# Linear attention with two expert layers on one core: the decay of the state moved from GpSimd to VectorE

## The chip, the cores and the metric

One core of a Trainium2 chip runs the whole program. A core has TensorE (PE in the profile; its weight loads are PEld), VectorE (DVE), ScalarE (ACT), GpSimd (POOL) and SyncE (SP, which issues the DMAs here). Each engine works through its own queue in order; semaphores tie the queues together. The metric is device time in microseconds, the median of several runs.

## What is computed

A linear attention with a complex, decaying state, then two expert layers on its output:

```python
for t in range(S):                      # q, k, v, a_re, a_im: [4, 8, 768, 48]
    ar, ai = a_re_n[:, :, t, :, None], a_im_n[:, :, t, :, None]
    new_re = ar * S_re - ai * S_im
    new_im = ar * S_im + ai * S_re
    kv = einsum('bhd,bhe->bhde', k[:, :, t], v[:, :, t])
    S_re, S_im = new_re + kv, new_im
    y[:, :, t] = einsum('bhd,bhde->bhe', q[:, :, t], S_re)
x = y.transpose(0, 2, 1, 3).reshape(3072, 384)
x = (silu(x @ w_gate) * (x @ w_val)) @ w_out      # 384 -> 1536 -> 384
h = x @ w_in                                      # 384 -> 2048
out = (h - tanh(h)) @ w_out2                      # -> 384
```

`a_re_n`, `a_im_n` are the inputs with their magnitude capped at 0.999.

## The kernel before

The 768 steps of each of the 4 batches are cut into 6 chunks of 128 steps. A batch and a chunk are a unit; there are 24, numbered 0 to 23, and chunk 0 of a batch begins with an empty state. Decay factors are prepared for two units at a time (`group_steps`: the magnitude's norm, a running complex product within the chunk on VectorE by `cstep`, L278 to L281, and at the end the small tile `LS` with the decay from one chunk's reference point to the next). `unit_a` scales q and k by the running products and sends them through DRAM to have them by head (`TQ`, `TK`). `unit_b` computes the unit's output: scores (`psS`, L434), the mask (L438 or L440), the outputs (`psY`: L462 with the scores, L466 with the state `Hn`), and the new state.

The state lies in a tile of 96 partitions: 48 rows of the real part, 48 of the imaginary part, and 384 columns (8 heads of 48). The step from one chunk to the next multiplies each row by the real factor of the decay, and adds the swapped halves (real and imaginary exchanged) times the imaginary factor. So a unit that is not the last of its batch computes `psG` (L446, what its keys and values add), adds the state it came with (L449 on VectorE; in chunk 0 ScalarE copies, L451) and gets `Z`; two DMAs on SP's queue (L453, L454) write `Z` with its halves exchanged into `Zs`. The next unit turns `Z` and `Zs` into `Hn` on GpSimd:

```python
POOL.tensor_tensor(out=heads(Hn), in0=heads(Z), in1=lam(0), op=ALU.mult)   # L427
POOL.tensor_tensor(out=heads(Zs), in0=heads(Zs), in1=lam(1), op=ALU.mult)  # L428
POOL.tensor_tensor(out=Hn, in0=Hn, in1=Zs, op=ALU.add)                     # L429
```

20 of the 24 units do that. `Z`, `Zs` and `Hn` have one buffer each, so a new `Hn` also waits for the matmuls that read the old one. GpSimd has besides these only the mask of the first eight units (L438) and two operations of the norm for ten groups (L241, L262).

The first expert layer (`moe1_tile`) runs over tiles of 2, 2, 2, 3, 3, 4, 4 and 4 units, each in 12 steps: 9 gate matmuls and 9 value matmuls (L581), silu on ScalarE (L585), the product (L590) and the split into a rounded part and a rest (L540 on ScalarE, L541 on VectorE), and 9 matmuls of `w_out` (L565). A tile can start when the outputs of its units are there. These steps are interleaved with attention. The second layer (`moe2_tile`, L645 and L668) comes after it and has TensorE for itself. Weights are decoded from 64-bit words by ScalarE and VectorE (L144 to L156).

The kernel is written in an order that mixes the steps by hand, and a scheduler then sets each engine's order by a simulated time line. So an edit of one operation can move others on all engines.

## Time and profile before

| | |
|---|---|
| median of 3 runs | 1235.29 us (1232.09 to 1238.32) |
| profiled execution | 1236.95 us, its span 1235.2 us |
| TensorE busy | 1091.5 us, 88% |
| VectorE busy | 985.6 us, 80% |
| ScalarE busy | 656.3 us, 53% |
| GpSimd busy | 128.2 us, 10% |
| mean granted clock of TensorE | 0.942 |

Busy shares are averages over stages with different limits, so they are read by stretch: attention and the first layer mixed (to about 640 us), the first layer's last tiles with little attention left (to about 740), then the rest of the first layer with the decode of the second layer's weights, and from about 850 us the second layer alone. An idle engine costs nothing where another sets the end; the chain of work that ended last tells which engine was waited for.

### The profile page before, as it was taken

What the parts mean: (1) busy time and instruction counts of PE and PEld (TensorE: products, weight loads), DVE (VectorE), ACT (ScalarE), POOL (GpSimd) and SP (SyncE); (2) the same over time, 40 slices, a digit from 0 to 9 for tenths busy, and PEclk for the clock granted to TensorE, in tenths of its full rate; (3) what the DMA queues carried; (4) which work ended last, traced back from release to release, by engine and by line L of the source; (5) the groups of instructions that cost most, each with busy time, mean ns of one, the idle gap of its engine ahead of it and who ended that gap; (6) DMA issues with size and microseconds to landing.
All of it is one profiled execution on the core that took longest, in us unless ns stands there. A gap on an engine that the chain in (4) does not pass through costs nothing.

```text
span 1235.2 us, 18483 instructions
## 1 busy us (share of the span) xinstructions
PE 1091.5 (88%) x6504; PEld 973.1 (79%) x6504; DVE 985.6 (80%) x2010; ACT 656.3 (53%) x1247; POOL 128.2 (10%) x110
## 2 busy tenths in 40 slices
PE   3157847879989999889999999989999999999997
PEld 1145847879988888878878888878999999999997
DVE  4888968866969778596885338989888888888886
ACT  5446537466464754536535224565565655555553
POOL 0011322202212122021111000000000000000000
PEclk9568977999989999889999999999999999999999
DMA  6397777897985978687667658652100102020000
GB/s 154 76 214 162 177 159 199 210 202 194 216 195 141 191 183 188 153 212 156 145 166 180 161 138 284 215 159 90 51 27 24 54 1 77 1 77 1 26 2 28
DMA packets 296707, 163.36 MB, mean 132 GB/s; under 512 B 157472, under 2 KB 273824, under 8 KB 296608
## 3 DMA queue, kind: packets, MB, share of 16 engines
q1 hardware_dynamic: 296608, 162.11, 52.3%
q8 instruction: 53, 0.87, 0.3%
q14 instruction: 46, 0.38, 0.1%
HBM read 111.82 MB, written 37.86 MB: 121 GB/s over the span
## 4 chain that ended last, share of the span: by engine, by line
PE 53%; DVE 17%; DMA 13%; ACT 9%; issue 3%; SPq 3%; POOL 0%; DVEq 0%; ACTq 0%
PE l L645 16%; PE l L668 15%; PE l L581 10%; PE acc L565 5%; DMA TQ<-qk_d 3%; PE psS L434 3%; DVE prod L278 3%; DVE PL L280 1%; DMA raw<-in_moe_w_out_dram 1%; DMA qk_d<-QK 1%; DMA TK<-qk_d 1%; PE psG L446 1%; DVE lo L541 1%; DVE t L590 1%; ACT PL L271 1%
## 5 line engine op out<-in xcount | busy, mean ns | idle before, releaser
L581 PE MATMUL l<-x,wgv 128*128 128x256 f32 (+2 forms) x1728 | 351.0, 350 | 10.8 <-ACT t L585 9.3
L581 PEld LDWEIGHTS l<-x,wgv 128*128 128x128 f32 x1728 | 284.8, 196 | 40.0 <-ACT t L585 12.7
L668 PE MATMUL l<-x,wi 128*128 128x512 f32 x864 | 215.1, 394 | 5.1 <-DVE t L611 5.1
L645 PE MATMUL l<-w,hi 128*128 128x384 f32 x768 | 189.7, 337 | 0.0
L668 PEld LDWEIGHTS l<-x,wi 128*128 128x128 f32 x864 | 161.9, 189 | 35.1 <-DVE t L611 6.2
L565 PE MATMUL acc<-hi,wo 128*128 128x256 f32 (+2 forms) x576 | 167.3, 351 | 9.1 <-ACT wo L154 4.1
L540 ACT CAST hi<-t 128x512 fp32r<-128x512 f32 (+2 forms) x192 | 108.6, 566 | 118.3 <-DVE t L590 87.4
L645 PEld LDWEIGHTS l<-w,hi 128*128 128x128 f32 x768 | 140.9, 189 | 7.4
L541 DVE TENSOR_TENSOR lo<-t,hi 128x512 fp32r<-128x512 f32 (+2 forms) x192 | 123.7, 645 | 26.7 <-ACT hi L540 26.5
L604 ACT ACTIVATE t<-l 128x512 f32<-128x512 f32 x96 | 57.3, 597 | 147.1 <-PE l L668 143.0
L645 PE MATMUL l<-w,lo 128*128 128x384 f32 x384 | 122.3, 337 | 0.0
L565 PEld LDWEIGHTS acc<-hi,wo 128*128 128x128 f32 x576 | 106.0, 196 | 20.1 <-ACT wo L154 5.1
L278 DVE TENSOR_TENSOR prod<-PL 128x384 f32<-128x384 f32 x168 | 104.8, 624 | 2.7
L565 PE MATMUL acc<-lo,wo 128*128 128x256 f32 (+2 forms) x288 | 98.5, 346 | 0.0
L434 PE MATMUL psS<-TQ,TK 96*128 96x128 f32 x384 | 61.8, 316 | 37.3 <-DMA TQ<-qk_d 19.5
L606 DVE TENSOR_TENSOR l<-l,t 128x512 f32<-128x512 f32 x96 | 67.1, 698 | 33.4 <-ACT uu L605 33.2
L434 PEld LDWEIGHTS psS<-TQ,TK 96*128 96x128 f32 x384 | 57.3, 225 | 42.6 <-issue 28.8
L590 DVE TENSOR_TENSOR t<-t,l 128x256 f32<-128x256 f32 (+2 forms) x96 | 52.6, 547 | 32.5 <-PE l L581 18.4
L585 ACT ACTIVATE t<-l 128x256 f32<-128x256 f32 (+2 forms) x96 | 47.1, 491 | 48.9 <-PE l L581 46.4
L611 DVE COPY_PREDICATED t<-far,l 128x512 f32<-128x512 int32 x96 | 71.0, 740 | 2.6
L610 DVE SCALAR_TENSOR_TENSOR t<-vv,t 128x512 f32<-128x512 f32 x96 | 66.2, 689 | 6.8
L645 PEld LDWEIGHTS l<-w,lo 128*128 128x128 f32 x384 | 71.4, 188 | 0.2 <-DVE lo L541 0.2
(129 smaller groups left out, 1670.8 us busy)
## 6 DMA issues: line engine op xcount, KB each, us to landing
wo<-wo_d SPq DMA_DIRECT2D x84, 384.0 KB, 3.9
qk_d<-QK SPq DMA_DIRECT2D x24, 768.0 KB, 4.7
TK<-qk_d SPq DMA_DIRECT2D x48, 192.0 KB, 4.2
TQ<-qk_d SPq DMA_DIRECT2D x48, 192.0 KB, 4.9
x<-o_d SPq DMA_DIRECT2D x12, 768.0 KB, 5.9
x<-y SPq DMA_DIRECT2D x48, 144.0 KB, 4.3
raw<-in_moe_w_in_dram SPq DMA_DIRECT2D x16, 384.0 KB, 4.1
raw<-in_moe_w_out_dram SPq DMA_DIRECT2D x16, 384.0 KB, 3.4
```

What stands on the lines that cost most here:

```text
L278: DVE.tensor_tensor(out=pr, in0=prev.unsqueeze(2).to_broadcast(sh), in1=cur.unsqueeze(1).to_broadcast(sh), op=ALU.mult)
L434: PE.matmul(ps[:, P * i:P * (i + 1)], lhsT=TK[:, 4 * hh + i], rhs=TQ[:, 4 * hh + i], start=True, stop=True)
L540: ACT.copy(out=hi, in_=t)
L541: DVE.tensor_tensor(out=lo, in0=t, in1=hi.bitcast(F32), op=ALU.subtract)
L565: PE.matmul(acc[j], lhsT=w[:, a, j * P:(j + 1) * P], rhs=m[b], start=(f == 0 and i == 0), stop=(f == NF1 - 1 and i == 2))
L581: PE.matmul(p, lhsT=w[a][:, kk], rhs=x[b][:, kk, 0:n_t], start=(n == 0), stop=(n == 3 * NJ - 1))
L590: DVE.tensor_tensor(out=s, in0=s, in1=ps[1], op=ALU.mult)
L606: DVE.tensor_tensor(out=p, in0=p, in1=t, op=ALU.subtract)
L610: DVE.scalar_tensor_tensor(out=t, in0=vv, scalar=G_F, in1=t, op0=ALU.add, op1=ALU.mult)
L611: DVE.copy_predicated(out=t, mask=far, data=p)
L645: PE.matmul(acc[tb], lhsT=g[a][:, tb * P:(tb + 1) * P], rhs=w2_hl[f][:, b], start=(f == 0 and n == 0), stop=(f == NF2 - 1 and n == 2))
L668: PE.matmul(p, lhsT=wi_hl[a][:, kk, sl], rhs=x[b][:, kk, :], start=(n == 0), stop=(n == 3 * NJ - 1))
```

## The change

The two planes `Z` and `Zs` become halves of one tile `ZZ` of 96 x 2 x 384. VectorE multiplies both planes in one instruction, in place, with the two factors of `LS` spread over the columns, and adds the planes into `Hn` in a second one. GpSimd no longer takes part. The state's sum, ScalarE's copy and the two DMAs stay, with the halves of `ZZ` as their targets.

```diff
-            Z = st.pop("Z")
-            Zs = st.pop("Zs")
+            ZZ = st.pop("Z")
             Hn = a1.tile([D2, DM], F32, tag="H", name="Hn")
-            lam = lambda x: LS[:, :, x, g].unsqueeze(2).to_broadcast([D2, H, D])
-            POOL.tensor_tensor(out=heads(Hn), in0=heads(Z), in1=lam(0), op=ALU.mult)
-            POOL.tensor_tensor(out=heads(Zs), in0=heads(Zs), in1=lam(1), op=ALU.mult)
-            POOL.tensor_tensor(out=Hn, in0=Hn, in1=Zs, op=ALU.add)
+            z4 = ZZ.rearrange("p c (h d) -> p c h d", h=H)
+            DVE.tensor_tensor(out=z4, in0=z4, in1=LS[:, :, :, g].rearrange("p h c -> p c h").unsqueeze(3).to_broadcast([D2, 2, H, D]), op=ALU.mult)
+            DVE.tensor_tensor(out=Hn, in0=ZZ[:, 0], in1=ZZ[:, 1], op=ALU.add)
...
-            Z = a1.tile([D2, DM], F32, tag="Z", name="Z")
+            ZZ = a1.tile([D2, 2, DM], F32, tag="Z", name="Z")
+            Z, Zs = ZZ[:, 0], ZZ[:, 1]
             if c > 0:
                 DVE.tensor_tensor(out=Z, in0=Hn, in1=ps[0:D2, 0:DM], op=ALU.add)
             else:
                 ACT.copy(out=Z, in_=ps[0:D2, 0:DM])
-            Zs = a1.tile([D2, DM], F32, tag="Zs", name="Zs")
             SP.dma_start(out=Zs[0:D], in_=Z[D:D2])
             SP.dma_start(out=Zs[D:D2], in_=Z[0:D])
-            st["Z"], st["Zs"] = Z, Zs
+            st["Z"] = ZZ
```

In the new file the lines behind the edit carry smaller numbers: the product is L426, the sum L427, the state's sum L448, the first layer's product L588 and its split L539, y L470.

GpSimd's queue in the middle of attention, before (L241 and L262 belong to the norm):

```order
L262 TENSOR_TENSOR ar<-ar,s_4911 128x768
L428 TENSOR_TENSOR Zs<-Zs,LS 96x384
L427 TENSOR_TENSOR Hn<-Z,LS 96x384
L429 TENSOR_TENSOR Hn<-Hn,Zs 96x384
L241 TENSOR_TENSOR s_5307<-s_5307,s_5308 128x768
```

The same queue in the changed kernel:

```order
L241 TENSOR_TENSOR s_4889<-s_4889,s_4890 128x768
L262 TENSOR_TENSOR ar<-ar,s_4889 128x768
L241 TENSOR_TENSOR s_5281<-s_5281,s_5282 128x768
L262 TENSOR_TENSOR ar<-ar,s_5281 128x768
L241 TENSOR_TENSOR s_6025<-s_6025,s_6026 128x768
```

The decay is gone from it and only the norm is left.

VectorE's queue around the state's sum before the decay of unit 10, before (L278 to L281 are the scan, L590 and L541 the first layer):

```order
L449 TENSOR_TENSOR Z<-Hn,psG 96x384
L280 TENSOR_TENSOR PL<-prod 128x96
L281 TENSOR_TENSOR PL<-prod 128x96
L278 TENSOR_TENSOR prod<-PL 128x384
L590 TENSOR_TENSOR t<-t,l_4295 128x384
```

The same place in the changed kernel:

```order
L448 TENSOR_TENSOR Z<-Hn,psG 96x384
L588 TENSOR_TENSOR t<-t,l_4010 128x384
L539 TENSOR_TENSOR lo<-t,hi 128x384
L299 MEMSET PL 128x6
L278 TENSOR_TENSOR prod<-PL 128x384
L280 TENSOR_TENSOR PL<-prod 128x96
L281 TENSOR_TENSOR PL<-prod 128x96
L278 TENSOR_TENSOR prod<-PL 128x384
L426 TENSOR_TENSOR Z<-Z,LS 96x768
L280 TENSOR_TENSOR PL<-prod 128x96
L281 TENSOR_TENSOR PL<-prod 128x96
L427 TENSOR_TENSOR Hn<-Z 96x384
```

Product and sum now stand in VectorE's queue among the scan's steps, the product seven rows behind the state's sum.

VectorE's queue at the state's sum before the decay of unit 22, before:

```order
L449 TENSOR_TENSOR Z<-Hn,psG 96x384
L590 TENSOR_TENSOR t<-t,l_7394 128x512
L541 TENSOR_TENSOR lo<-t,hi 128x512
L472 TENSOR_TENSOR y<-psY,y 128x4x128
L590 TENSOR_TENSOR t<-t,l_7432 128x512
```

The same place in the changed kernel, with the semaphores each instruction waits for (DMAHW are DMA queues):

```order
L448 TENSOR_TENSOR Z<-Hn,psG 96x384 [waits PE_49]
L426 TENSOR_TENSOR Z<-Z,LS 96x768 [waits DMAHW3_49,DMAHW2_49,DMAHW4_49,DMAHW1_49,DVE_49]
L588 TENSOR_TENSOR t<-t,l_7392 128x512 [waits PE_49,Activation_49]
L539 TENSOR_TENSOR lo<-t,hi 128x512 [waits Activation_49]
L427 TENSOR_TENSOR Hn<-Z 96x384 [waits PE_49]
L470 TENSOR_TENSOR y<-psY,y 128x4x128 [waits DMAHW6_49,DMAHW3_49,DMAHW7_49,DMAHW0_49,Activation_49]
```

The product stands right behind the state's sum, ahead of the first layer's product and split.

## Rows read from the trace of the kernel before

**Rows 1.** The page: busy time of each engine, and the chain that ended last.

```profile
PE 1091.5 (88%) x6504; PEld 973.1 (79%) x6504; DVE 985.6 (80%) x2010; ACT 656.3 (53%) x1247; POOL 128.2 (10%) x110
...
PE 53%; DVE 17%; DMA 13%; ACT 9%; issue 3%; SPq 3%; POOL 0%; DVEq 0%; ACTq 0%
```

**Rows 2.** Busy time by stretch: length, engines (instructions), clock, DMA share, GB/s.

```profile
92.00:640.00 548.00, 474.84 (x3409) 435.77 (x3407) 441.53 (x1008) 304.73 (x603) 111.03 (x84) 0.93 0.77 181
640.00:850.00 210.00, 204.89 (x1068) 170.34 (x1067) 147.32 (x311) 93.67 (x173) 9.39 (x9) 0.98 0.64 187
```

**Rows 3.** Groups by line and shape: busy us, mean ns, idle before and releasers.

```profile
L390 DVE TENSOR_TENSOR QK<-qk,NW 128x768 f32<-128x768 f32 x48 | 47.1, 989 | 6.3 <-ACT qk L385 4.5 <-DMA qk_d<-QK 1.9
...
L427 POOL TENSOR_TENSOR Hn<-Z,LS 96x384 f32<-96x384 f32 x20 | 23.4, 1172 | 72.3 <-DVE prod L278 23.2 <-DMA LS<-lam_d 22.2 <-issue 13.3
...
L429 POOL TENSOR_TENSOR Hn<-Hn,Zs 96x384 f32<-96x384 f32 x20 | 22.6, 1130 | 1.5
...
L428 POOL TENSOR_TENSOR Zs<-Zs,LS 96x384 f32<-96x384 f32 x20 | 20.1, 1006 | 176.7 <-DMA Zs<-Z 143.8 <-DVE t L590 25.0 <-DVE T L335 7.7
...
L261 DVE SCALAR_TENSOR_TENSOR ai<-ai,sgn,s 128x768 f32<-128x768 f32 x12 | 17.2, 1430 | 0.0
...
L156 DVE TENSOR_TENSOR wi<-t,wi 128x384 fp32r<-128x384 f32 x16 | 8.8, 553 | 0.1
```

**Rows 4.** Instructions in order of time: start, duration, engine, line; VectorE beside GpSimd.

```profile
92.91 1.16 POOL L427 TENSOR_TENSOR Hn<-Z,LS 96x384 f32<-96x384 f32 x1
93.29 1.20 DVE L146 TENSOR_SCALAR dt<-dt 128x768 int32<-128x768 int32 x1
...
96.47 1.19 POOL L429 TENSOR_TENSOR Hn<-Hn,Zs 96x384 f32<-96x384 f32 x1
...
107.56 0.55 DVE L146 TENSOR_SCALAR dt<-dt 128x768 int32<-128x768 int32 x1
...
715.19 0.69 DVE L472 TENSOR_TENSOR y<-psY,y 128x512 fp32r<-128x512 f32 x1 [3.12 <-ACT y L468]
...
716.52 1.00 POOL L429 TENSOR_TENSOR Hn<-Hn,Zs 96x384 f32<-96x384 f32 x1
```

**Rows 5.** GpSimd's waits before L428 (us, times), and three pairs in time order.

```profile
  DMA Zs<-Z: 143.8, 13
...
221.18 0.54 DVE L449 TENSOR_TENSOR Z<-Hn,psG 96x384 f32<-96x384 f32 x1
...
224.73 0.94 POOL L428 TENSOR_TENSOR Zs<-Zs,LS 96x384 f32<-96x384 f32 x1 [4.83 <-DMA Zs<-Z]
...
472.88 0.54 DVE L449 TENSOR_TENSOR Z<-Hn,psG 96x384 f32<-96x384 f32 x1
...
480.91 0.84 POOL L428 TENSOR_TENSOR Zs<-Zs,LS 96x384 f32<-96x384 f32 x1 [2.63 <-DMA Zs<-Z]
...
683.22 0.55 DVE L449 TENSOR_TENSOR Z<-Hn,psG 96x384 f32<-96x384 f32 x1 [2.53 <-issue]
...
689.28 0.84 POOL L428 TENSOR_TENSOR Zs<-Zs,LS 96x384 f32<-96x384 f32 x1 [18.61 <-DMA Zs<-Z]
```

**Rows 6.** VectorE's work of the cover: two groups; two lines with min/median/max ns.

```profile
L541 DVE TENSOR_TENSOR lo<-t,hi 128x384 fp32r<-128x384 f32 x24 | 14.9, 620 | 4.5 <-ACT hi L540 4.5
...
L590 DVE TENSOR_TENSOR t<-t,l 128x384 f32<-128x384 f32 x24 | 13.1, 547 | 3.4 <-ACT t L585 2.7 <-PE l L581 0.7
...
L278 DVE TENSOR_TENSOR prod<-PL x168: 540/557/3031, 31.7 to 647.7; 128x384 f32<-128x384 f32 x168
...
L280 DVE TENSOR_TENSOR PL<-prod x168: 242/257/1983, 32.3 to 648.3; 128x96 f32<-128x96 f32 x168
```

**Rows 7.** In order of time: the first matmul that reads a decayed state.

```profile
102.71 0.39 PE L466 MATMUL psY<-TQ,Hn 96*48 96x128 f32 x4
```

**Rows 8.** A stretch with the last units, and one step's matmuls, in order of time.

```profile
675.00:700.00 25.00, 25.00 (x159) 21.07 (x158) 9.21 (x14) 5.98 (x12) 2.69 (x3) 1.00 0.69 173
...
730.15 4.25 PE L581 MATMUL l<-x,wgv 128*128 128x512 f32 x18
```

## The prediction

> **What bounds the kernel now.** I read the page first (busy time by engine, the chain of work that ended last), then the busy times by stretch. TensorE is busy 88% of the span and VectorE 80%; GpSimd, which loses work here, only 10%. Of the chain VectorE holds 17% and GpSimd 0% [rows 1]. So what the change takes from GpSimd shortens no chain by itself, and what it puts on VectorE can lengthen one. The stretches say where: up to 640 us attention and the first expert layer run mixed, TensorE idles 73 of 548 us, VectorE 106 of 548, and the pace is set by attention's steps passing from engine to engine; from 640 us to 850 TensorE is busy 205 of 210 us [rows 2]. All 20 decays lie between 92.9 and 717.5 us (the first operation starts at 92.91, the last at 716.52 [rows 4]), 17 of them before 640. All that the change can do to the time, it does through VectorE's queue in the mixed stretch, or by keeping TensorE waiting later.
>
> **The work removed.** GpSimd loses 20 times three operations: 1.17, 1.01 and 1.13 us each, 66.1 us [rows 3]. Nobody was near them: the new state was ready 5.0 us before its first reader in the closest of the 20 cases (its sum ends at 96.47 + 1.19 = 97.66 us, the matmul starts at 102.71) and 7 to 32 us before it in the 19 others [rows 4, 7]. A shorter decay is therefore worth nothing to the chain; I count 0 for it.
>
> **The work added.** VectorE gains 20 products of 96x768 and 20 sums of 96x384. The nearest row for the product is L390, 128x768 with an operand spread over two planes: 0.99 us mean, and 0.95 us where no other engine stretched it. The sum's nearest row is L156, both operands in SBUF: 0.55 us [rows 3]. I take 0.95 + 0.55 = 1.50, times 20 = 30 us. The upper bound of the product is L261, 1.43 us [rows 3], which makes 40 us; the lower bound is the 0.95 itself.
>
> **What VectorE gets back.** VectorE is slowed while GpSimd computes. L146 on 128x768 takes 0.55 us when GpSimd is idle and 1.20 us when it meets the decay's product [rows 4]. I went through all VectorE instructions that overlap one of the 60 decay operations: 86, from the L146 at 93.29 to the L472 at 715.19 us [rows 4], each against the lower quartile of its own line and shape. 40 of them are over 0.1 us too long, mostly by 0.53 to 0.87 us, and the sum is 25.0 us. That goes away with the operations. So VectorE's work rises by 30 - 25 = 5 us only, from 985.6 to about 991 us.
>
> The Trainium skill (SBUF — State Buffer, section "SBUF: two separate sides") has a rule for this: VectorE and GpSimd share one port pair as an exclusive lock, so that a VectorE instruction with two SBUF inputs stands still while a GpSimd operation holds it. The trace agrees in kind: the 0.65 us by which L146 is stretched is more than half of the 1.16 us of the GpSimd operation beside it [rows 4]. By the rule alone the removal could give back up to the whole 66.1 us, and the balance would be 30 - 66 = -36 us instead of +5.
>
> **The wait that moves.** The product needs both planes, so it waits for the two copies that swap the state's halves (two DMAs on SP's queue). Before, GpSimd stood in that wait, 143.8 us in 13 cases [rows 5], and nothing was queued behind it but GpSimd's own few operations. Now VectorE stands in it, in order, and what is queued behind is the first layer's product and split (L588, L539 of the new file), the scan's steps and y. From the state's sum to the landing of the copies it took 3.0 us at best (221.72 to 224.73), 7.5 us at worst (473.42 to 480.91), 5.5 us in the PE-bound part (683.77 to 689.28); the mean over the cases where nothing but the copies was missing is 5.2 us, of which these are the two ends and one [rows 5].
>
> The order of the changed kernel puts some VectorE work between the state's sum and the product. In 11 units of the mixed stretch there are 5 to 18 rows there. At the place shown in the order it is a product and split of the first layer and four operations of the scan: 0.55 + 0.62 + 2 x 0.56 + 2 x 0.26 = 2.8 us [rows 6]. In the same way the 11 covers are 2.6 to 7.1 us, together 43 us. With 5.2 us of landing each, the uncovered rest is 16 us; with 3.0 us everywhere it is 1 us, with 7.5 us it is 39 us. I take 16, by the mean. In the six others of the mixed stretch the cover is over 13 us, or the state comes from ScalarE's copy and not from VectorE; I count 0 for these.
>
> In the last three units the cover is 1.6, 0 and 0 us, so by the same mean VectorE will stand 3.6 + 5.2 + 5.2 = 14 us there. But TensorE is busy 25.00 of 25 us there and VectorE only 9.2, and behind the state's matmuls TensorE has the next step's gate and value matmuls of the first layer in its queue, 18 of them in 4.25 us [rows 8], which need nothing of the blocked product. I count 0 for it; if that cover fails it is 1 to 2 us a unit, 5 us in all.
>
> **The sum.** VectorE's queue in the mixed stretch grows by 5 us of work and 16 us of waits, 21 us. How much reaches the end? VectorE's share of the chain is 17% of 1235 = 210 us, and behind 850 us the chain is almost TensorE alone, so it held 210/850 = 25% of the chain where it matters. 21 x 0.25 = 5 us. The bounds of that share are 0 (its 106 idle us swallow all) and its busy share, 442/548 = 81% [rows 2], which makes 17 us. The profiled execution took 1236.95 us for a span of 1235.2, and the median of the runs is 1235.29, 1.7 us under that execution; against the median the forecast is 1235.3 + 5 = 1240 us. About 0.5%, 6.2 us, is what a measurement of this kernel can tell from no change.
>
> **The order of everything else.** The change also shifts the scheduler's order on TensorE: before the scores of units 2 to 7, 0 to 3 steps of the first layer more stand ahead than before, before units 10 to 15 up to 1 step less. Before unit 15's outputs both have 60 of 96 steps, the whole of what is ready then. So I expect gaps to move, not to vanish, and price the shift at 0, with some 5 us either way for the range.
>
> **The rivals.**
> *The lock gives more than it costs (faster).* If VectorE was held not for 25 us but for most of the 66.1 us (instructions that were not yet started, and so show no stretch), its queue changes by 30 - 66 + 16 = -20 us at the mean wait, or -35 us with the shortest landing. Times 0.25 that is -5 to -9 us: 1226 to 1230. For it: every stretch seen is near the length of the GpSimd operation. Against: a held instruction would show as a long one, and I summed those.
> *VectorE stands in the copies' wait (slower).* The product is the first instruction of VectorE that waits for those transfers, with the scan's steps behind it, on which the next group's attention hangs. If most of the 21 us reaches the end, at the busy share of 81%, it is +17: 1252 us; it decides against the kernel from a share of 30% on (6.2/21). For it: 7 of the 11 covers are under 4 us, and SP's queue is often behind. Against: the 106 idle us that VectorE has anyway.
> *The product is no single cheap pass.* If the spread operand makes it 1.43 us as in L261, VectorE gets 10 us more, at 25% 2.5 us: 1243. This lies inside the slower case.
>
> **How the numbers follow.** Forecast (change of -6 to +6, likeliest +5): 0.42. The lock, or a luckier order, by more than 0.5%: 0.24, at about 1228. The wait on the copies: 0.34, at about 1250. The likeliest case's own range is 1230 to 1241. The range that leaves 2 in 10 out reaches to the ends of both rivals: 1226 to 1254. Faster by over 0.5%: 0.24; within: 0.42; slower: 0.34.
>
> **What would show it.** In the changed kernel's profile: the product at 0.95 us and the sum at 0.55 us, 20 of each; GpSimd at 62 us instead of 128; VectorE at 988 to 1001 us busy, with far fewer L278 and L280 instructions over 1 us; VectorE's waits with the copies as the releaser of the product, 10 to 40 us in the mixed stretch and near 14 us behind 640 us; TensorE still gapless between 640 and 740 us. The forecast is wrong if the gapless stretch of TensorE begins more than 10 us before or behind 640 us, or if the waits for the copies exceed 40 us, or if TensorE gets gaps behind the product in the last three units.

## The result, and the profile after

The changed kernel takes 1250.36 us (median of 6 runs, 1245.31 to 1253.62), the kernel before 1234.31 us beside it on the same chip. The ratio is 1.0109 with a 95% interval of 1.0089 to 1.0129: **slower by 1.1%, some 14 us**. The forecast was 1240 us and no measurable change; the time lies in the range and not where it was put.

The page of the changed kernel, engines and chain, answers to [rows 1]; the two stretches answer to [rows 2]:

```profile
PE 1097.3 (88%) x6504; PEld 977.7 (78%) x6504; DVE 986.3 (79%) x2050; ACT 661.1 (53%) x1249; POOL 56.1 (4%) x50
...
PE 55%; DVE 14%; DMA 14%; ACT 9%; SPq 4%; issue 3%; POOL 0%; DVEq 0%; ACTq 0%
```

```profile
92.00:640.00 548.00, 469.52 (x3324) 431.66 (x3325) 428.24 (x1009) 305.49 (x596) 49.80 (x33) 0.92 0.75 176
640.00:850.00 210.00, 203.75 (x1100) 169.56 (x1099) 148.48 (x322) 89.72 (x169) 0.00 (x0) 0.99 0.66 191
```

GpSimd lost 72 us (66 of them the decay), VectorE gained 0.7 us in all, and VectorE's share of the chain fell from 17% to 14%. So the chain that ended last has less of the engine that got the work and more of TensorE (55%, before 53%). TensorE is busy 5.3 us less in the mixed stretch than before and 12.3 us more behind 850 us (390.52, before 378.18). Not all of this is work that moved: over the whole span it is busy 5.8 us more for the same 6,504 matmuls, and idle 7.9 us more, which together is the span's 13.7 us.

The new operations by line and shape (they stand at L426 and L427; lines behind them are 2 smaller than before's):

```profile
L426 DVE TENSOR_TENSOR Z<-Z,LS 96x768 f32<-96x768 f32 x20 | 19.3, 966 | 27.9 <-DMA Z<-Z 25.4 <-DMA ar<-in_a_re_dram 1.5 <-DMA LS<-lam_d 1.0
L427 DVE TENSOR_TENSOR Hn<-Z 96x384 f32<-96x384 f32 x20 | 12.6, 628 | 0.1
```

Product 0.97 us, sum 0.63 us, and 27.9 us of waiting ahead of the product, nearly all for the two copies. All of this is near the forecast. What was not forecast stands in TensorE's waits of the mixed stretch (us in all, times, longest), here after:

```profile
PE psS L432 <- DMA TQ<-qk_d: 23.2, 10, 6.5
PE acc L563 <- DMA wo<-wo_d: 19.6, 13, 5.3
```

and the same two of the kernel before:

```profile
PE psS L434 <- DMA TQ<-qk_d: 12.9, 6, 4.4
...
PE acc L565 <- DMA wo<-wo_d: 1.8, 3, 1.0
```

TensorE waits 42.8 us instead of 14.7 for two kinds of transfer, the turned queries and the w_out weights, that neither the product nor the sum touches. (Both tables are of 92 to 640 us.) They show which wait came last and not how much was lost: all idle time of TensorE in this stretch rose by 5.3 us only, from 73.2 to 78.5, since other waits shrank.

The loss shows better between the outputs of units 4 and 12, first before, then after (columns as in [rows 2]):

```profile
229.30:458.70 229.40, 205.91 (x1577) 198.44 (x1576) 179.33 (x432) 130.12 (x263) 42.48 (x34) 0.96 0.82 195
```

```profile
241.50:470.40 228.90, 196.05 (x1479) 187.53 (x1478) 173.40 (x427) 125.32 (x246) 19.57 (x14) 0.94 0.78 181
```

The changed kernel comes to unit 4's output 12.2 us later, but with 956 matmuls behind it instead of 863, and TensorE was idle 92.1 us up to there, before 94.7. So far work was moved ahead, and TensorE lost nothing to gaps. The next eight units then take the same 229 us with 98 matmuls fewer: TensorE is idle 32.8 us instead of 23.5, and its granted clock is 0.94 instead of 0.96. From the last unit's output to the end the changed kernel needs 500.2 us, before 504.4, and wins 4.2 us back.

The first large delay can be followed to unit 2's q and k products (L390). Before, VectorE:

```profile
117.86 0.96 DVE L365 SCALAR_TENSOR_TENSOR NW<-NW,x 128x768 f32<-128x768 f32 x1
...
123.52 0.95 DVE L390 TENSOR_TENSOR QK<-qk,NW 128x768 f32<-128x768 f32 x1
```

After, first ScalarE and then VectorE:

```profile
117.88 1.28 ACT L583 ACT_TABLE_LOAD   x1
119.17 0.39 ACT L583 ACTIVATE t<-l 128x256 f32<-128x256 f32 x1
119.58 1.28 ACT L362 ACT_TABLE_LOAD   x1
120.87 0.94 ACT L362 ACTIVATE x<-NW,tiny 128x768 f32<-128x768 f32 x1
```

```profile
126.07 0.95 DVE L426 TENSOR_TENSOR Z<-Z,LS 96x768 f32<-96x768 f32 x1 [0.98 <-DMA LS<-lam_d]
...
127.28 0.95 DVE L365 SCALAR_TENSOR_TENSOR NW<-NW,x 128x768 f32<-128x768 f32 x1
...
133.78 0.95 DVE L390 TENSOR_TENSOR QK<-qk,NW 128x768 f32<-128x768 f32 x1
```

The second of the unit's two products comes 10.3 us later. In ScalarE's queue the first layer's first SiLU now stands ahead of the group's normalisation, with a table load on either side; in VectorE's queue the decay stands ahead of the normalisation's last step. Neither is a longer instruction. Both are places in a queue.

### The profile page after: what moved, and what is told of

Its sections match the earlier page's. It is cut to its first block, busy times and chain, and to the rows that moved or that the text cites. A ratio compares the mean times of both kernels' runs of the same rounds, so it can differ in the third digit from the quotient of the medians.

```text
span 1248.9 us, 18400 instructions
## 1 busy us (share of the span) xinstructions
PE 1097.3 (88%) x6504; PEld 977.7 (78%) x6504; DVE 986.3 (79%) x2050; ACT 661.1 (53%) x1249; POOL 56.1 (4%) x50
## 4 chain that ended last, share of the span: by engine, by line
PE 55%; DVE 14%; DMA 14%; ACT 9%; SPq 4%; issue 3%; POOL 0%; DVEq 0%; ACTq 0%
PE l L643 15%; PE l L666 15%; PE l L579 12%; PE acc L563 6%; DMA TQ<-qk_d 3%; DMA wo<-wo_d 3%; DVE prod L278 2%; PE psS L432 2%; DMA Z<-Z 2%; DMA qk_d<-QK 2%; DMA x<-in_moe_w_val_dram 1%; PE psG L444 1%; DVE lo L539 1%; DMA ar<-in_a_re_dram 1%; DMA x<-y 1%
## 5 line engine op out<-in xcount | busy, mean ns | idle before, releaser
L579 PEld LDWEIGHTS l<-x,wgv 128*128 128x128 f32 x1728 | 286.6, 198 | 43.7 <-ACT t L583 10.5
L539 DVE TENSOR_TENSOR lo<-t,hi 128x512 fp32r<-128x512 f32 (+2 forms) x192 | 126.1, 657 | 30.4 <-ACT hi L538 30.1
L563 PEld LDWEIGHTS acc<-hi,wo 128*128 128x128 f32 x576 | 106.5, 197 | 36.7 <-DMA wo<-wo_d 22.9
L278 DVE TENSOR_TENSOR prod<-PL 128x384 f32<-128x384 f32 x168 | 98.2, 584 | 2.7
L588 DVE TENSOR_TENSOR t<-t,l 128x256 f32<-128x256 f32 (+2 forms) x96 | 52.7, 548 | 39.7 <-PE l L579 30.5
```

The source lines that it names most:

```text
L278: DVE.tensor_tensor(out=pr, in0=prev.unsqueeze(2).to_broadcast(sh), in1=cur.unsqueeze(1).to_broadcast(sh), op=ALU.mult)
L539: DVE.tensor_tensor(out=lo, in0=t, in1=hi.bitcast(F32), op=ALU.subtract)
L563: PE.matmul(acc[j], lhsT=w[:, a, j * P:(j + 1) * P], rhs=m[b], start=(f == 0 and i == 0), stop=(f == NF1 - 1 and i == 2))
L579: PE.matmul(p, lhsT=w[a][:, kk], rhs=x[b][:, kk, 0:n_t], start=(n == 0), stop=(n == 3 * NJ - 1))
```

## The experiments

Two theories. **V**: the product, the sum and the wait for the copies themselves cost the time, in VectorE's queue. **O**: they cost little, and the time goes through the other order that the scheduler makes on every engine once VectorE has 40 instructions more. In the two orders another instruction stands at 1,167 of VectorE's 2,011 places and at 3,174 of TensorE's 5,782 (the decay left out).

To part them, an order was written out as edges, one from each instruction of an engine to the next, so that the scheduler has no choice left but for the decay's own instructions. The order of either kernel can so be given to the other, whole or up to a point in time. In the expectations S (start) and G (group 2's scan) name places for the loss of the order, W (whole) says that it is spread over all of it. A late output is not yet lost time, as the two stretches above show; it says how far attention is behind.

All runs: ratio to the kernel before on the same chip; then how much later (us) than in the trace of before the output y of a unit is done (before: 155.9, 229.3, 320.1, 458.7, 561.7, 670.5 us), and the span.

| run | operations, order | ratio (95%) | y2 | y4 | y7 | y12 | y16 | y20 | span |
|---|---|---|---|---|---|---|---|---|---|
| after | new, its own | 1.0109 (1.0089–1.0129) | 8.5 | 12.2 | 8.9 | 11.8 | 17.4 | 17.8 | 1248.9 |
| e1 | new, before's | 1.0021 (1.0004–1.0038) | 2.3 | 0.7 | 0.1 | -0.2 | -0.5 | -0.3 | 1235.4 |
| e2 | old, after's | 1.0095 (1.0075–1.0115) | 8.4 | 12.0 | 11.2 | 10.9 | 11.4 | 9.7 | 1241.0 |
| e3 | new on GpSimd, free | 1.0031 (1.0013–1.0049) | -1.1 | 0.0 | -0.8 | 0.8 | 1.0 | 0.8 | 1234.5 |
| e4 | new, before's to 165 | 1.0105 (1.0082–1.0127) | 1.4 | 10.3 | 6.6 | 9.5 | 13.5 | 15.5 | 1246.7 |
| e5 | new, after's to 173 | 1.0050 (1.0032–1.0069) | 9.0 | 1.8 | -0.9 | 1.8 | 0.5 | 0.8 | 1235.8 |
| e6 | new, after's, 2 moves | 1.0133 (1.0109–1.0156) | 12.6 | 14.8 | 10.2 | 12.1 | 15.5 | 17.3 | 1248.5 |
| e7 | new, 2 edges, free | 1.0308 (1.0278–1.0338) | 13.3 | 25.0 | 30.3 | 24.2 | 36.1 | 35.4 | 1271.7 |
| e8 | new, before's to 200 | 1.0138 (1.0115–1.0161) | 2.9 | 13.6 | 10.9 | 12.6 | 16.2 | 17.2 | 1248.3 |
| e9 | new, after's 165–214 | 1.0140 (1.0113–1.0166) | 0.7 | 8.4 | 12.8 | 11.8 | 10.5 | 10.5 | 1247.0 |
| e10 | new, 1 edge, free | 1.0219 (1.0197–1.0241) | 8.8 | 5.1 | 15.0 | 13.0 | 21.3 | 22.9 | 1259.0 |
| e11 | sum on VectorE, free | 1.0078 (1.0054–1.0101) | 6.2 | 4.2 | 5.8 | 4.4 | 9.0 | 6.6 | 1240.5 |
| e12 | new, before's to 310 | 1.0066 (1.0043–1.0088) | 1.9 | -0.7 | 2.7 | 3.2 | 9.5 | 9.4 | 1240.5 |
| e13 | new, before's to 430 | 1.0039 (1.0021–1.0058) | 3.2 | 1.7 | 2.2 | 4.3 | 9.4 | 9.4 | 1240.4 |
| e14 | new, after's to 444 | 1.0129 (1.0101–1.0157) | 9.5 | 12.9 | 8.1 | 12.6 | 12.9 | 13.5 | 1249.6 |
| e15 | old, 1 edge, free | 0.9994 (0.9973–1.0014) | -0.2 | 1.9 | 6.2 | 0.6 | 0.9 | -1.7 | 1229.3 |
| e16 | new, after's, scan moved | 1.0147 (1.0114–1.0180) | 9.5 | 21.0 | 21.4 | 20.9 | 25.2 | 26.8 | 1258.0 |
| e17 | three on VectorE, free | 1.0166 (1.0123–1.0208) | 9.5 | 11.8 | 6.7 | 11.5 | 16.9 | 13.5 | 1251.6 |
| e18 | new, e15's | 1.0069 (1.0041–1.0097) | 1.1 | 0.0 | 3.9 | -2.0 | -0.2 | 4.3 | 1235.4 |

### Operations against order: e1, e2, e3

e1 is the changed kernel with the order of before. The edit (the order itself is a packed list of some 10,000 characters):

```diff
         tile_kernel(tc, *args)
+        keep_order(tc, nc)
...
+def keep_order(tc, nc):
+    runs = json.loads(zlib.decompress(base64.b85decode(ORDER)))
...
+    for e, rr in runs.items():
+        seq = [by[e][a + k] for a, n in rr for k in range(n)]
...
+        for x, y in zip(seq, seq[1:]):
+            tc.add_manual_dep(y, x.name, info, reason="order")
```

> The changed kernel (product and sum on VectorE), but every other instruction of each engine is issued in the order that it had in the kernel before; only where the 40 new instructions stand among VectorE's others is left to the scheduler. Theory O (the 15 us are lost through the other order that the scheduler gives all engines): the time is that of before, 1229 to 1240 us, although the product and the sum take their 0.95 and 0.55 us and VectorE waits for the copies as in the changed kernel (some 13 waits, 15 to 40 us). Theory V (the lost time is the product, the sum and the wait for the copies themselves, standing in VectorE's queue): it is that of the changed kernel, 1247 to 1254 us, and the outputs of the units fall behind by some 17 us between 110 and 530 us as there.

e2 is the kernel before with the same lines, and in ORDER the order of the changed kernel.

> The kernel before (three operations on GpSimd), but every other instruction of each engine is issued in the order that it has in the changed kernel. Theory O: it is as slow as the changed kernel, 1245 to 1254 us, with 15 to 25 us of TensorE's waits for the w_out loads, as there. Theory V: it is as fast as the kernel before, 1230 to 1239 us, since VectorE has neither the new work nor the wait. If both theories hold in part, this run and the one with before's order stand on either side of the middle, near 1242 us.

Measured: e1 1236.65 us (1.0021), e2 1245.05 us (1.0095). The changed kernel's 1.09% is 0.21% of operations and 0.95% of order, within the intervals. **Theory V falls, theory O holds.** The trace of e1 shows why V falls: the product waits for the copies there too, 18.7 us in 13 cases, and the price of all is the 0.21%. By line of e1:

```profile
L426 DVE TENSOR_TENSOR Z<-Z,LS 96x768 f32<-96x768 f32 x20 | 19.3, 967 | 20.5 <-DMA Z<-Z 18.7 <-DMA TK<-qk_d 1.9
```

TensorE's two waits go with the order and not with the operations, first in e1, then in e2:

```profile
PE psS L432 <- DMA TQ<-qk_d: 10.7, 5, 2.8
...
PE acc L563 <- DMA wo<-wo_d: 2.8, 4, 1.1
```

```profile
PE psS L434 <- DMA TQ<-qk_d: 20.4, 9, 5.8
PE acc L565 <- DMA wo<-wo_d: 15.8, 9, 4.8
```

How the order's loss reaches the end is another matter, and here TensorE's clock comes in. Between the outputs of units 4 and 12 in e2:

```profile
241.30:469.60 228.30, 201.09 (x1488) 192.49 (x1487) 174.56 (x417) 125.19 (x247) 36.56 (x32) 0.92 0.80 184
```

The granted clock is 0.92, before 0.96. Over the whole of its profiled execution e2's TensorE is idle no longer than before (143.4 and 143.7 us) and busy 6.1 us longer for the same matmuls, which is the whole of the 5.8 us between these two spans. The other runs agree: e2's were granted 0.938 to 0.943 on the mean, those of before beside them 0.944 to 0.951, e1's 0.944 to 0.953. In the changed kernel's profiled execution the clock over the whole is 0.944, before 0.942, so there the order's loss is not one of clock on the whole; but its six runs reach from 0.936 to 0.944. Whether the lower clock follows from where the gaps lie, no run here shows.

e3 leaves both operations on GpSimd:

```diff
-            DVE.tensor_tensor(out=z4, in0=z4, in1=LS[:, :, :, g]..., op=ALU.mult)
-            DVE.tensor_tensor(out=Hn, in0=ZZ[:, 0], in1=ZZ[:, 1], op=ALU.add)
+            POOL.tensor_tensor(out=z4, in0=z4, in1=LS[:, :, :, g]..., op=ALU.mult)
+            POOL.tensor_tensor(out=Hn, in0=ZZ[:, 0], in1=ZZ[:, 1], op=ALU.add)
```

> The new form (both planes in one tile, one product, one sum), but both operations on GpSimd, with the scheduler free. Its order differs from before's in few places. Both theories: the time of before, 1231 to 1239 us, since GpSimd's operations are on no chain; the product takes 1.9 to 2.4 us on GpSimd (two halves of 1.0 to 1.2), the sum 1.13 us. If it is 1245 us or more, the layout of the two planes in one tile itself costs, and both theories are wrong.

Measured: 1237.82 us (1.0031); the rows of its trace differ from before's at 29 of VectorE's 2,010 places. The layout and the form cost no more than 0.5%, and two operations instead of three on GpSimd were worth nothing, as [rows 7] had it. On GpSimd the product takes 1.63 us, below the 1.9 to 2.4 expected.

### Where the order loses: e4 to e6 and e7

e4 and e5 use e1's lines with other orders: before's up to 165 us and the changed kernel's from there, and the changed kernel's up to 173 us and before's from there.

```
e4: ORDER = before's rows that start ahead of 165 us, then the rest as in the changed kernel
e5: ORDER = the changed kernel's rows that start ahead of 173 us, then the rest as in before
```

> The changed kernel's operations; up to 165 us (just behind the output of unit 2) each engine issues its instructions in the order of before, from there on in the order of the changed kernel. Theory S (start): the order loses its time where unit 2's q and k products come 11.6 us later on VectorE (132.44 against 120.87 us), and the rest of the order is as good as the other: unit 2's output at 156 to 159 us, the time 1236 to 1241 us. Theory W (whole): the loss of the order is spread over the whole mixed stretch, and the start carries little: unit 2's output is early here too, but units 12 to 20 are again 8 us or more behind before, and the time is 1244 to 1251 us.

> The reverse: the changed kernel's operations, up to 173 us the order of the changed kernel, from there on that of before. Theory S: unit 2's output at 164 us, and the 8 us stay to the end: 1243 to 1249 us. Theory W: the units catch up with before between 173 and 640 us: 1235 to 1241 us.

Measured: e4 1247.23 us (1.0105), e5 1240.54 us (1.0050), both in the range of W. **Theory S falls.** e4 has a good start (y2 1.4 us late) and falls back by 8.9 us between units 2 and 4; e5 has the bad start (9.0 us late) and has won it back by unit 4. Unit 2's late products, the first delay that the eye meets in the trace, cost about 0.3% (e5 against e1). What e4 does between 165 and 194 us stands on VectorE; L349 is the last of group 2's lambdas, on which units 4 and 5 hang:

```profile
169.16 0.56 DVE L145 TENSOR_SCALAR dt<-dt 128x768 f32<-128x768 f32 x1 [5.85 <-ACT dt L144]
...
193.98 0.15 DVE L349 TENSOR_TENSOR lam<-lp 128x6 f32<-128x6 f32 x1
```

and in e1, with before's order:

```profile
183.03 0.16 DVE L349 TENSOR_TENSOR lam<-lp 128x6 f32<-128x6 f32 x1
```

VectorE stands 5.85 us before the decoding of a weight tile whose data are not there, and the last steps of group 2's scan stand behind it: the next one starts at 182.00 us, in e1 at 163.28. In the changed kernel's order 20 of the 24 weight tiles are decoded ahead of these lambdas, in before's 17. The Trainium skill (PSUM — Partial Sum Buffer, section "Engine vs sequencer instructions") says that the queues of ScalarE, VectorE and GpSimd are strictly first in, first out; the row of e4 agrees, a ready step waited 5.85 us behind one that was not.

e6 moves two things in the changed kernel's order: the SiLU with its table loads behind the normalisation, and unit 2's decay behind its q and k products.

```diff
 ORDER (ScalarE)
-L583 SiLU, L362, L144, L363
+L362, L144, L363, L583 SiLU
 VectorE
+tc.add_manual_dep(prog["prod", G], prog["qk", G].name, NoSync)
```

> The changed kernel in its own order, with two moves in the start: on ScalarE the first layer's first SiLU stands behind the normalisation of group 1 instead of ahead of it (two loads of the activation table, 1.28 us each, and the 0.39 us SiLU leave the chain to unit 2's q and k products), and on VectorE the decay's product and sum of unit 2 stand behind these products instead of ahead (0.95 + 0.98 waiting for the lambdas + 0.55 us). Theory S by these two alone: the q and k products come 5 us earlier, at 127 us, unit 2's output at 159 us, and the time is 1244 to 1247 us. If the time stays at 1248 to 1252 us although the products are 5 us earlier, something else in this stretch's order holds unit 2 (the first-layer steps that stand ahead of its scores on TensorE).

Measured: 1250.23 us (1.0133), y2 even later (12.6 us). Unit 2's two products came at 132.96 and 134.29 us instead of 132.44 and 133.78. The wait had only moved: the first layer's product, which needs the SiLU that now comes later, kept its place in VectorE's queue ahead of the normalisation's last steps, and VectorE stood before it:

```profile
124.60 0.42 DVE L588 TENSOR_TENSOR t<-t,l 128x256 f32<-128x256 f32 x1 [7.79 <-ACT t L583]
```

So the two rows alone do not hold the products, and what they cost was not taken out by this run.

e7 gives the same two edges to the free scheduler:

```diff
+tc.add_manual_dep(prog["silu"], prog["norm", G].name, NoSync)
+tc.add_manual_dep(prog["prod", G], prog["qk", G].name, NoSync)
```

> The changed kernel with the same two orders given to the scheduler as edges (first SiLU behind group 1's normalisation, unit 2's product behind its q and k products), all else left to the scheduler, which then makes yet another order behind them. Theory S: unit 2's output at 155 to 160 us and 1237 to 1244 us. Theory W: any time between 1235 and 1253 us, and no relation between unit 2's output and the end.

Measured: 1272.34 us (1.0308), outside both forecasts. The order that the scheduler makes behind these two edges costs 2% more than the one that they were to mend.

### One place or many: e8 to e11

Theory G: three more tiles decoded ahead of group 2's scan are the cause. e8 and e9 are again splices; e10 and e11 are free orders with 17 tiles ahead.

```
e8: ORDER = before's rows that start ahead of 200 us, then the rest as in the changed kernel
e9: ORDER = before's to 165 us, the changed kernel's to 214 us, then before's
```

> As the run with before's order up to 165 us, but with the cut at 200 us, behind unit 4's q and k products; the changed kernel's order from there. Theory G: the order loses its time in one place, on VectorE between 165 and 190 us, where the decoding of three more weight tiles (20 instead of 17) stands ahead of the last steps of group 2's scan, so that group 2's lambdas come at 194 instead of 183 us and everything after keeps that distance. Then unit 4's output is at 229 to 231 us and the time 1235 to 1241 us. Theory W (the loss is spread over the whole order): 1242 to 1249 us, with unit 12's output 5 us or more behind before.

> The reverse: before's order everywhere but between 165 and 214 us, where it is that of the changed kernel (three more tiles decoded on VectorE ahead of group 2's lambdas). The operations are the changed kernel's. Theory G: unit 4's output at 237 to 241 us, some 10 us late, and most of that stays to the end: 1242 to 1249 us. Theory W: the units catch up and it is 1235 to 1240 us.

Measured: e9 1250.12 us (1.0140), y4 8.4 us late, as G has it (the time 1 us above its range): this stretch alone costs as much as the whole order. Its trace shows little of that as gaps: TensorE is idle 145.0 us, before 143.7, and busy 1102.0 us instead of 1091.5, at a granted clock of 0.935 instead of 0.942. But e8, where group 2's lambdas are on time, is 1250.81 us (1.0138), above both forecasts: y4 is 13.6 us late. Group 3's lambdas come at 257.6 us there, in e1 at 245.9, so in e8 it is the next group that falls back. At 200 and 214 us the two orders have begun different work (15 instructions of TensorE's 540 at 200 us), so each splice has a seam of its own in it.

e10 holds the 17th tile's decoding, in the changed kernel with the scheduler free:

```diff
+tc.add_manual_dep(decoded[16], lams[2].name, NoSync)
```

> The changed kernel with the scheduler free but for one edge: on VectorE the decoding of the 17th weight tile may not start ahead of group 2's lambdas. In the order that it makes, 17 tiles are decoded ahead of them, as before (the changed kernel: 20). Theory G: unit 4's output at 229 to 234 us, the time 1234 to 1242 us. Theory W: the scheduler's order is another one everywhere else, so any time between 1236 and 1272 us.

e11 leaves the sum alone on VectorE (the second line as in the changed kernel):

```diff
-            DVE.tensor_tensor(out=z4, in0=z4, in1=LS[:, :, :, g]..., op=ALU.mult)
+            POOL.tensor_tensor(out=z4, in0=z4, in1=LS[:, :, :, g]..., op=ALU.mult)
```

> The new form, but only the sum on VectorE; the product of both planes on GpSimd. The scheduler is free and its order differs from before's by 726 of 2,031 rows on VectorE, but 17 tiles are decoded ahead of group 2's lambdas. Theory G: about as fast as before, 1232 to 1241 us, in spite of the other order, and unit 4's output at 228 to 234 us. Theory W: as far from before as the changed kernel, 1243 us or more.

Measured: e10 1260.77 us (1.0219), e11 1242.80 us (1.0078), both with 17 tiles ahead and both slower than G allows (e11 by 1.8 us, with unit 4's output where G had it). In e10 unit 4 is 5.1 us behind and unit 7 already 15.0. **The count of tiles does not make an order good**; theory G is not enough.

### Clean cuts, and an order that is only other: e12 to e15

At 310 us the two orders have issued the same work but for 9 instructions, at 430 us (444 us in the changed kernel) but for one.

```
e12: ORDER = before's rows that start ahead of 310 us, then the rest as in the changed kernel
e13: the same with 430 us
e14: ORDER = the changed kernel's rows that start ahead of 444 us, then the rest as in before
```

> The changed kernel's operations; before's order up to 310 us, the changed kernel's order from there. At this point both orders have issued the same work on each engine up to 9 instructions, which was not so at 200 us. Theory G (the order loses in the start, where it lets the first layer run ahead of attention): unit 7's output at 319 to 322 us, units 8 to 23 at most 5 us behind before, 1236 to 1242 us. Theory W (spread): 1243 to 1248 us, with units 12 to 20 falling behind by 6 us or more.

> As the run before it, with the cut at 430 us, where the two orders have issued the same instructions but for one transfer. Theory G: the time of the changed operations in before's order, 1235 to 1240 us. Theory W: the last third of the mixed stretch still costs 3 to 6 us (units 12 to 20 fall behind in this stretch): 1239 to 1243 us.

> The reverse of the last: the changed kernel's order up to 444 us (unit 11's output), before's from there. Theory G: the whole loss is there, unit 12's output 10 to 12 us behind before, and it stays: 1246 to 1251 us. Theory W: part of it is won back, 1240 to 1245 us. With the cut at 430 us the two halves of the loss should add up to the whole (some 13 to 14 us over before).

Measured: e14 1250.35 us (1.0129), as G has it; e13 1240.40 us (1.0039), in the range of W; e12 1242.18 us (1.0066), 0.2 us above the range of G, with units 16 and 20 further behind than it allows. Over e1's 1.0021, the order up to 444 us costs 1.1%, the whole loss; the order behind 430 us 0.2%, which the intervals do not part from nothing; the order behind 310 us 0.45%. So the net loss arises in the front of the mixed stretch. e8 and e12 differ only in the rows between 200 and 310 us, and e8 is 0.7% slower; with e9 that makes the stretch of groups 2 and 3, from 165 to 310 us, the costly one. The parts do not add up: e5, e9 and e12, whose stretches hardly overlap, cost 0.3 + 1.2 + 0.45%, twice the whole. (The back of the order is not harmless to attention either: in e12 and e13 unit 20 is 9.4 us late and the span only 5 us longer, since behind unit 23 they need 500 us where before needs 504.) TensorE's waits in e14:

```profile
PE psS L432 <- DMA TQ<-qk_d: 28.2, 9, 6.2
PE acc L563 <- DMA wo<-wo_d: 13.1, 10, 5.0
```

e15 is the kernel before with one edge, on the same tile as e10:

```diff
+tc.add_manual_dep(decoded[16], lams[2].name, NoSync)
```

> The kernel before, its three operations on GpSimd, with one edge for the scheduler: on VectorE the 17th weight tile's decoding may not start ahead of group 2's lambdas. No operation is changed or added, and one tile fewer is decoded ahead of them (16 instead of 17). If fewer decodings ahead of the scan are what makes an order good: unit 4's output at 224 to 229 us and 1226 to 1236 us. If before's order is a good one among many, because the kernel's numbers were chosen on it, any other order is worse whatever edge makes it: 1239 to 1262 us.

Measured: 1233.16 us, 0.9994 (0.9973 to 1.0014), though another instruction stands at 998 of VectorE's places and 2,615 of TensorE's than in before. So an order is not slow merely for being another than the one on which the kernel's numbers were chosen. One such order does not show that good ones are common: of the other free orders e3's is nearly before's own, and those of the changed kernel, e7, e10, e11 and e17 are slower.

### The scan alone, a third form, and the operations in a second order: e16 to e18

e16 is the changed kernel in its own order, with 41 rows of VectorE and 10 of ScalarE moved:

```diff
 ORDER (VectorE)
+L278, L280, L281 (six steps of group 2's scan), L333 to L349
 L145 (18th tile)
 ...
-L278, L280, L281 (six steps of group 2's scan), L333 to L349
 ORDER (ScalarE)
-L326, L327, L359, L360, L362, L363 of group 2, behind the 21st tile's L144
+L326, L327, L359, L360, L362, L363 of group 2, behind unit 3's y
```

> The changed kernel in its own order but for 41 rows of VectorE and 10 of ScalarE: the last six scan steps and the lambdas of group 2 stand ahead of the decoding of the 18th weight tile instead of behind the 20th, and the normalisation of group 2 follows them. TensorE's, GpSimd's and SP's orders are the changed kernel's. Theory G (the decoding ahead of the scan is the cause): the lambdas come at 178 to 184 instead of 195.9 us, unit 4's output 5 to 10 us earlier than the changed kernel's 240.8 us, and the time 1240 to 1245 us. If the lambdas come early but unit 4's output and the time stay (1248 to 1252 us), the places of unit 4's pieces behind three more first-layer steps on TensorE hold it as well, and no single engine's order is the cause.

Measured: 1252.21 us (1.0147), its interval (1.0114 to 1.0180) overlapping that of the changed kernel. The profiled execution took 1259.73 us, the slowest of the six, so its lateness is more than is usual for e16. The move did what it should to the lambdas and nothing for the units; VectorE of e16:

```profile
185.23 0.16 DVE L349 TENSOR_TENSOR lam<-lp 128x6 f32<-128x6 f32 x1
...
215.81 0.36 DVE L145 TENSOR_SCALAR dt<-dt 128x384 f32<-128x384 f32 x1 [2.26 <-ACT dt L144]
...
218.48 1.82 DVE L390 TENSOR_TENSOR QK<-qk,NW 128x768 f32<-128x768 f32 x2
```

beside the changed kernel:

```profile
195.92 0.16 DVE L349 TENSOR_TENSOR lam<-lp 128x6 f32<-128x6 f32 x1
...
212.31 1.82 DVE L390 TENSOR_TENSOR QK<-qk,NW 128x768 f32<-128x768 f32 x2
```

The lambdas come 10.7 us earlier (1 us behind the range given), unit 4's q and k products 6.2 us later. The likely reading is that the scan's time was taken from the decodings, that the first layer's steps wait for these, and that unit 4's pieces stand behind the same steps in the same queues; the waits in the trace fit it, and no run holds it apart. Of the expectation the second branch is the nearer one, although unit 4's output did not stay but came 8.8 us later still: the scan's place in VectorE's queue alone is not the cause.

e17 takes before's three lines, with VectorE:

```diff
-            POOL.tensor_tensor(out=heads(Hn), in0=heads(Z), in1=lam(0), op=ALU.mult)
-            POOL.tensor_tensor(out=heads(Zs), in0=heads(Zs), in1=lam(1), op=ALU.mult)
-            POOL.tensor_tensor(out=Hn, in0=Hn, in1=Zs, op=ALU.add)
+            DVE.tensor_tensor(out=heads(Hn), in0=heads(Z), in1=lam(0), op=ALU.mult)
+            DVE.tensor_tensor(out=heads(Zs), in0=heads(Zs), in1=lam(1), op=ALU.mult)
+            DVE.tensor_tensor(out=Hn, in0=Hn, in1=Zs, op=ALU.add)
```

> The old three operations, all on VectorE, the scheduler free. In its order 20 tiles are decoded ahead of group 2's lambdas, as in the changed kernel. VectorE gets 3 x 0.55 = 1.65 us a unit, 33 us, instead of 30. Theory G: unit 4's output at 238 to 243 us and 1246 to 1255 us. If it is 1235 to 1242 us, 20 tiles ahead do not cost what I say.

Measured: 1253.65 us (1.0166), with y4 11.8 us late, as expected of an order with 20 tiles ahead. With e10 in view this is in keeping with G and does not prove it.

e18 is the changed kernel with e1's lines and e15's order.

> The changed kernel's operations in the order of the run in which before had one edge (its time was that of before, with 16 tiles ahead of group 2's lambdas). The price of the product and the sum in VectorE's queue was 2.6 us in before's order; if it does not hang on the order, this is 1234 to 1239 us, and the changed kernel is as fast as before to within 0.4% once the order is a good one. If it is 1243 us or more, the operations cost what they meet, and the price in before's order was luck.

Measured: 1241.10 us (1.0069), between the two forecasts. Against e15 the operations cost 0.75% here, some 9 us (0.4 to 1.1% by the two intervals), against 0.21% in before's order and 0.14% in the changed kernel's own (after against e2). Its profiled execution (span 1235.4) is the fastest of its runs, so the trace does not show where those 9 us lie.

## Why the prediction was wrong

Point by point, by its own steps:

- **The work removed, 0 on the chain**: right. e3 does with two operations what took three and gains nothing.
- **The work added, 0.95 + 0.55 us, 30 us**: right; 0.97 + 0.63 us, 31.9 us.
- **Given back, 25 us of VectorE's stretch**: right in kind and size. VectorE's busy time rose by 0.7 us where 5 were forecast; the durations of its instructions added up, which counts overlaps twice, rose by 4.0 us. The stretch that is left beside GpSimd stems from the norm's L241 and L262, some 26 us as before, the 25 us of the decay are gone. The balance of -36 us by the rule of the Trainium skill (SBUF — State Buffer, section "SBUF: two separate sides") did not come. The L146 that the prediction set beside that rule has one input and not two, so it is no instance of the rule as put there.
- **The wait that moves, 16 us mixed and 14 behind 640 us**: right; 15.0 us (12.5 for the copies, 1.5 and 1.0 for other transfers) and 12.9 us. TensorE got no gap behind the product in the last three units. It was not gapless from 640 us on, though: a first-layer tile waits for attention's outputs until 661.86 us, 22 us behind that, where before the last gap ahead of 740 us ends at 620 us. This is one of the signs of being wrong that the prediction named, and it points at the order:

```profile
661.86 4.36 PE L579 MATMUL l<-x,wgv 128*128 128x512 f32 x18 [2.20 <-DMA x<-y]
```

- **The sum, 21 us times 0.25**: about right as the price of the operations. e1 gives 2.6 us (0.5 to 4.7) in before's order where 5 were forecast, after against e2 some 2 us, e18 against e15 about 9 us in a third order.
- **The order of everything else, priced at 0 with 5 us either way**: this step failed. e2, which has nothing of the change but its order, is 11.7 us slower. The step compared one count, first-layer steps ahead of a unit's scores on TensorE, saw it come out even by unit 15, and took it that gaps move and keep their size. The count was right: 93 matmuls more stand ahead of unit 4's output, which comes 12.2 us later, with TensorE 14.7 us longer at work up to there. But the count came out even by doing less later and not by doing it faster: the next eight units took 229 us as before, with 98 matmuls fewer, 9.3 us more idle time of TensorE and a lower clock. That attention sets the length of such a stretch is argued and not shown: the units come in groups of two, each group's scan, normalisation and products pass through VectorE, ScalarE, SP and TensorE in turn, and each of these queues is in order. A count on one queue says little of the others.

The rival "VectorE stands in the copies' wait" gave 1252 us, and 1250 was measured. That is luck: e1 has that wait and not that time. That 1250 lies in the range is luck too, since the range took its upper end from this rival.

What is shown: the order costs 0.95%, the operations 0.1% to 0.75%, depending on the order that they stand in; the order's net loss arises ahead of 444 us and is not the price of every other order. What stays open: which rows make it, how much of it goes through TensorE's clock, and why. Two removals of suspects (e6, e16) moved the wait to other rows, the splices do not add up, and no count of rows that was tried tells good orders from bad ones. One column of the table parts them after the fact: where y4 is at most 1.9 us late, the ratio is at most 1.0069, where it is 4.2 us late or more, at least 1.0078 (the two nearest, e18 and e11, are not clear of each other). That is a sign and not a cause. No version beat the kernel before; e15 is its equal.

## What to carry to other kernels

Where a scheduler lays out several in-order queues, moving 40 instructions to another engine is a change of the whole order, and its price is a term of its own, here 11.7 us against 2.6 for the instructions. It can be measured apart: give the new operations the old order, and the old operations the new one. A wait or a row that looks guilty in the trace is a suspect until it alone has been moved, and the trace of that run must show that the wait is gone and has not moved to the next row, as it did in e6. And a piece of work that comes late is no loss by itself: what counts is what the busiest engine did meanwhile, in gaps, in work and in granted clock.

## What the runs showed of the hardware

- A load of ScalarE's activation table takes 1.28 us, and the next activation starts with it done, at 119.17 us behind a load at 117.88. All 42 loads in the changed kernel's trace take 1.28 us and begin 0.02 us behind the end of the instruction ahead of them. The Trainium skill (ScalarE: Activation LUTs, section "What ACT_TABLE_LOAD costs") gives 1283 ns for the load, which agrees, and 1380 ns more for a drain, which these rows do not show.
- GpSimd's product of 96x768 in one instruction takes 1.63 us (e3), its two products of 96x384 took 1.17 + 1.01 us [rows 3]; its sum took 1.23 us there and 1.13 before.
